# Quarters of the queries for the heads of the last two pairs: the end of a fused attention, routed feed-forward and gate kernel

## The chip, the cores and the metric

The kernel runs on one core of one Trainium2 chip. The metric is the device time of one execution in microseconds; the time before is the median of three runs.

## The reference

With x of 2048 rows (queries) and 512 columns, 32 heads of 16 values each:

```
qkv = x @ wqkv;  scores = q k^T / 4;  p = softmax(scores);  a = concat_heads(p v) @ wo
r = x @ w_r;  idx = the 2 rows of x with the largest r
y = ((silu(x[idx] @ w_gate) * (x[idx] @ w_up)) @ w_down) * sigmoid(r[idx])
b = x, with y added to the rows idx
g = sigmoid((x * gate_w).sum(-1))
out = g * a + (1 - g) * b
```

The softmax is over all 2048 keys, without a mask. The change touches the attention of the last two pairs of heads and the product with wo that follows it.

## The kernel before, in words

**Units and steps.** The heads are taken in 16 pairs. A unit is one pair and one half of the queries (1024), so there are 32 units, `u = 2 * pair + half`. A unit has 16 steps, one for each block of 128 keys: 512 steps in all. `Kx` holds the K of a pair (two buffers, by the pair's parity), `Qx` the queries of a unit (three buffers); each head has its own half of the partitions. `load_q` and `load_k` fetch them from scratch memory two units ahead (`start_step`).

**Three passes, interleaved.** For each unit the kernel first needs the largest score of each query. `m_piece` (line 546) makes one product of 128 queries by 512 keys on TensorE, 64 for a unit, and VectorE reduces them (line 560). GpSimd splits the result in a high and a low part (`pool_split`, lines 74 and 75), VectorE transposes it (line 610), and eight small transfers put it into two further rows of `Qx` (line 615), so that the scores come out with the maximum subtracted. `s_piece` (line 617) makes the scores of 128 keys by 512 queries (line 624) four times a step, and ScalarE takes their exponential (line 625). `av_mm` multiplies them by V and by a column of ones (line 633): `AV` then holds, for four blocks `ct` of (head, 512 queries), 16 rows of values and one row of sums. `av_out` copies it out at the end of a unit.

**The order** is written out by hand. While there are max products, one cycle of `ORDER` has twelve `s` (three steps), twelve `m`, three `A` (`p_v`, the value products of a step, two steps behind) and one `f`, which takes the next entry of a queue of other TensorE work (`slots`). The max products run 21 steps ahead, so they end near step 491. From step 492 on, a plain loop does four scores, one `p_v` and one entry of the queue in each step. `at_step(s, f)` hangs a function on the end of step `s`. All transfers but the indirect ones are issued by SyncE, in the order of the program.

**The output.** Heads are grouped by eight, four groups of 128 rows. For the first three, the values go to scratch, are divided by the sums and multiplied with wo in the queue (`wo_groups`). The fourth group ends with the last pair and is handled at the end. The values of pairs 12 to 14 (96 rows) go straight into `last_n`, one tile for each half of the queries. Their sums collect in `Lt`, which `l_out` inverts in eight slices on VectorE (`l_out`, line 667) and writes out; `l_last` reads them back, spread over 16 rows each, and `n_last` multiplies on GpSimd. `split_last` splits them into high and low parts (lines 524 and 525), and `wo_last` (line 534) makes one output tile of 128 queries: three matmuls (`wo_terms`, line 481) and the addition to `acc` on VectorE (`finish`, line 529). Tiles 8 to 15 do this with 96 rows, from step 497 on. For the last pair's first half (unit 30), the sums are turned and inverted by TensorE and VectorE (`l_cols` and `l_rows`, lines 684 and 693, the latter multiplied in at line 695), and its rows then join `last_n[0]`, which gives tiles 0 to 7 with all 128 rows; six of them at the ends of steps 506 to 511, two in `tail`. The last unit ends in `tail`: its sums are turned (line 721), inverted (723), spread (729, 730), turned back (733) and multiplied in (736); then eight output tiles of three matmuls each with `wz` (line 749), a copy of the last pair's rows of wo set between zeros, and for each an addition (529) and a store (532).

Of the kernel before, what the change touches and what calls it, by code (L numbers as in the profile page):

```python
# [23 lines left out]
STEPS = UNITS * KT  # L24
EL = 64


# [6 lines left out]
def gated_mix(ctx: ExitStack, tc: tile.TileContext, xT, x, wqkv, wo, w_rg, w_gate, w_up, w_down,  # L34
# [67 lines left out]
    i_scr = dram.tile([128, 1], U32, name="i_scr")  # L102
    r_scr = dram.tile([4 * 128, 128], F32, name="r_scr")


# [132 lines left out]
    def load_k(pair):  # L238

        g, r = divmod(pair * 32, 128)  # L240
        for j in range(2):
            o = (g * 128 + r + 16 * j) * S
            t = Kx[pair % 2].bitcast(F32)
            nc.sync.dma_start(t[64 * j:64 * j + 32, :], ap(qk_scr["k"], o, [[S, 16], [D * S, 2], [1, S]]).bitcast(F32))
            nc.sync.dma_start(t[64 * j + 32:64 * j + 48, :], ap(qk_scr["k"], o, [[S, 16], [1, S]]).bitcast(F32))

    def load_q(u):

        pair, half = divmod(u, 2)
        g, r = divmod(pair * 32, 128)  # L250
        n = S // 2
        for j in range(2):
            o = (g * 128 + r + 16 * j) * S + half * n
            t = Qx[u % 3].bitcast(F32)
            nc.sync.dma_start(t[64 * j:64 * j + 32, :], ap(qk_scr["q"], o, [[S, 16], [0, 2], [1, n]]).bitcast(F32))
            nc.sync.dma_start(t[64 * j + 32:64 * j + 48, :], ap(qk_scr["q"], D * S + o, [[S, 16], [1, n]]).bitcast(F32))

# [192 lines left out]
    wop = []  # L450
# [62 lines left out]

    def split_last(half, q):
        if q == 0:
            if half:
                t = ring.tile([128, 2, 1024], F32R, tag="xs", name="lahl", bufs=2)
                lastp[half] = t[:, 0], t[:, 1]
            else:
                lastp[half] = [xp.tile([128, 1024], F32R, tag=f"xl{i}", name="lahl") for i in (2, 3)]  # L520
        k = 128 if half == 0 else 96
        sl = slice(q * 512, q * 512 + 512)
        hi, lo, src = lastp[half][0][:k, sl], lastp[half][1][:k, sl], last_n[half][:k, sl]
        nc.vector.tensor_copy(hi, src)
        nc.gpsimd.tensor_sub(lo, src, hi.bitcast(F32))

# [19 lines left out]
    def m_piece(g):  # L546

        u, e = divmod(g, EL)
        t, c, j = e // 8, e // 2 % 4, e % 2
        r = g % 3  # L550
        if r == 0:
            MX[0] = mxa_tile()
        elif r == 2:
            MX[1] = mxb_tile()
        dst = MX[0][:, r] if r < 2 else MX[1]
        nc.tensor.matmul(dst, Qx[u % 3][64 * j:64 * j + 48, t * 128:t * 128 + 128],  # L556
                         Kx[(u // 2) % 2][64 * j:64 * j + 48, c * 512:c * 512 + 512], start=True, stop=True)
        if r:
            g0 = (g - 1 if r == 1 else g) % (3 * EL)
            nc.vector.tensor_reduce(Mr[:, g0:g0 + (2 if r == 1 else 1)], MX[r - 1], axis=AX.X, op=OP.max, negate=True)  # L560
# [56 lines left out]
    def s_piece(s, j, c):  # L617
        u, kt = divmod(s, KT)
        if s not in P:
            P[s] = ring.tile([128, 4, 512], F32, tag="P", name="P", bufs=3)  # L620
        k = Kx[(u // 2) % 2][64 * j:64 * j + 50, kt * 128:kt * 128 + 128]
        q = Qx[u % 3][64 * j:64 * j + 50, c * 512:c * 512 + 512]
# [4 lines left out]
    def av_mm(s):  # L627
# [3 lines left out]
        for ct in range(4):  # L631
            h = (u // 2) * 2 + ct // 2
            nc.tensor.matmul(AV[0][32 * ct:32 * ct + 32, :], V[:, kt, h * VW:h * VW + 32], P[s][:, ct, :],  # L633
                             start=kt == 0, stop=kt == KT - 1)
# [4 lines left out]
    def av_out(u):  # L639
# [24 lines left out]
    def l_out(g, i):  # L664
        n = 96 if g == 3 else 128
        sl = slice(16 * i, 16 * i + 16)
# [4 lines left out]
    def l_last(half, q):  # L671

        r = o_tile("rb", [96, 512])
        nc.sync.dma_start(r, ap(r_scr, 3 * 8 * S + half * 1024 + q * 512, [[S, 6], [0, 16], [1, 512]]))
        AV["rb", half, q] = r

    def n_last(half, q):
        a = last_n[half][:96, q * 512:q * 512 + 512]
        nc.gpsimd.tensor_mul(a, a, AV["rb", half, q])

    def l_cols(u):
        ps = mxa_tile()[:, 0, :16]
        for c in range(4):
            nc.tensor.matmul(ps[:, 4 * c:4 * c + 4], AV[u][:, c * 128:c * 128 + 128], sel_l, start=True, stop=True)
        r = ring.tile([128, 16], F32, tag="r16", name="r16", bufs=2)
        nc.vector.reciprocal(r, ps)
        AV["rx"] = o_tile("rx", [128, 16, 32])
        nc.vector.tensor_copy(AV["rx"], r[:, :, None].to_broadcast([128, 16, 32]))

    def l_rows(u):  # L690
        ps = mxa_tile()[:, 0]
        for c in range(4):
            nc.tensor.matmul(ps[:, c * 128:c * 128 + 128],
                             AV["rx"][:, 4 * c:4 * c + 4].rearrange("p a b -> p (a b)"), ident, start=True, stop=True)
        nc.vector.tensor_mul(AV[u], AV[u], ps)

    def last_rows():
        for ct in range(4):
            j, c = divmod(ct, 2)
            nc.sync.dma_start(last_n[0][96 + 16 * j:112 + 16 * j, c * 512:c * 512 + 512], AV[UNITS - 2][32 * ct:32 * ct + 16, :])  # L700

    wz = []

    def load_wz(part):
        if part == 0:
            wz.append(ring.tile([128, 2, 2, 512], F32R, tag="xs", name="wz", bufs=2))
            nc.gpsimd.memset(wz[0].bitcast(F32), 0.0)
            return
        for i in range(2):
            for ct in range(4):  # L710
                j, c = divmod(ct, 2)
                nc.sync.dma_start(wz[0][32 * ct:32 * ct + 16, i, c].bitcast(F32),
                                  wop[i][96 + 16 * j:112 + 16 * j, 3].bitcast(F32))

    def tail():
# [28 lines left out]
        for c in range(4):  # L744
            sl = slice(c * 128, c * 128 + 128)
            for k in range(2):
                ps = (st_tile, lambda: two[:, 0], st_tile, mxb_tile, st_tile, lambda: two[:, 1], st_tile, fl_tile)[2 * c + k]()
                for n, (a, b) in enumerate(((0, 0), (1, 0), (0, 1))):
                    nc.tensor.matmul(ps, hl[a][:, sl], wz[0][:, b, k, :], start=n == 0, stop=n == 2)
                finish(8 + 4 * k + c, ps)  # L750
                store(8 + 4 * k + c)

# [38 lines left out]
    def slots():  # L791
# [53 lines left out]
    at_step(400, load_wz, 0)  # L845
    at_step(404, load_wz, 1)

    def p_v(s):
# [7 lines left out]
        if u % 8 == 7 and u < 24:  # L856
            for i in range(8):
                at_step(s + 6 + i, l_out, u // 8, i)
        elif u == UNITS - 3:
            for i in range(8):  # L860
                at_step(s + 3 + i // 2, l_out, 3, i)
            for half in (1, 0):
                for q in range(2):
                    at_step(s + 10 - half, l_last, half, q)
                    at_step(s + 12 - half, n_last, half, q)
        elif u == UNITS - 2:
            at_step(s + 1, l_cols, u)
            at_step(s + 2, l_rows, u)
            at_step(s + 3, last_rows)

    def start_step(s):
        now[0] = s
        u = s // KT + 2
        if s % KT == 0 and u < UNITS:
            if u % 2 == 0 and u > 2:
                load_k(u // 2)
# [88 lines left out]
```

## Time and profile before

| | before |
|---|---|
| median of 3 runs | 1443.08 us (1442.3 to 1449.25) |
| the profiled execution | 1443.71 us, span 1441.9 us |
| TensorE busy | 1426.5 us, 99% of the span |
| VectorE busy | 1300.1 us, 90% |
| ScalarE busy | 1168.7 us, 81% |
| GpSimd busy | 302.5 us, 21% |
| mean granted TensorE clock | 0.998 |

In the profile's lines PE is TensorE, PEld its weight loads, DVE VectorE, ACT ScalarE, POOL GpSimd, and SP SyncE; a q after the name is the engine's own queue (issues and waits). A row of the timeline has its start and length in us, the engine, the line of the kernel, the operation, what is written and read, the shape and the count. In a row of groups the numbers behind the bar are the busy time in us and the mean of one in ns, then the idle time before them and what ended it. In a row of stretches the bounds and the length are followed by the busy us of PE, PEld, DVE, ACT and POOL with the count of instructions in brackets. In the chain of waits each row has a start and the share of time that the path to the end spent there.

### The profile page before, as it was taken

The numbers are of one execution on the slowest core, as the hardware profiler recorded it, in microseconds if no ns is written. First come the engines' busy times: TensorE is split into PE (matmuls) and PEld (weight loads), VectorE is DVE, ScalarE is ACT, GpSimd is POOL, SyncE is SP. The second block draws the span as 40 slices with busy tenths as digits, with TensorE's granted clock in tenths as the row PEclk, the third lists the DMA queues.
The fourth block names the chain that finished last, engine by engine and source line by source line (L and its number), as shares of the span: only waits on it lengthen the run. The fifth ranks groups of instructions, "written<-read, shape, count | busy, mean of one in ns | idle before, by whom it ended". The sixth has DMA issues, their size and how long they took to land.

```text
span 1441.9 us, 24169 instructions
## 1 busy us (share of the span) xinstructions
PE 1426.5 (99%) x9141; PEld 631.9 (44%) x9141; DVE 1300.1 (90%) x1541; ACT 1168.7 (81%) x2262; POOL 302.5 (21%) x321
## 2 busy tenths in 40 slices
PE   8999999999999999999999999999999999999998
PEld 5654444444444444444444443434444444444434
DVE  5779999999999999999999999999999999999933
ACT  4468888888888888888888888888888888888874
POOL 3652000112000001200001100033832222233220
PEclk9999999999999999999999999999999999999999
DMA  8702021212214121312222342314213121111003
GB/s 265 195 21 64 20 52 31 53 45 41 53 53 107 61 53 31 67 31 64 57 81 52 98 104 70 86 42 130 73 31 68 35 53 27 32 31 38 25 17 117
DMA packets 53475, 92.71 MB, mean 64 GB/s; under 512 B 12972, under 2 KB 24300, under 8 KB 51856
## 3 DMA queue, kind: packets, MB, share of 16 engines
q1 hardware_dynamic: 53264, 91.17, 24.4%
q8 instruction: 72, 1.18, 0.4%
q14 instruction: 43, 0.35, 0.1%
q0 software_dynamic: 96, 0.01, 0.0%
HBM read 63.64 MB, written 28.56 MB: 64 GB/s over the span
## 4 chain that ended last, share of the span: by engine, by line
PE 95%; DMA 2%; DVE 1%; SPq 1%; ACT 0%; issue 0%; POOL 0%; DVEq 0%; POOLq 0%; ACTq 0%
PE av L633 35%; PE st L624 23%; PE mxa L556 12%; PE mxb L556 10%; PE fl L150 6%; PE fl L481 4%; PE st L268 3%; DMA xs<-xT 1%; PE mxa L583 1%; DVE Mr L560 1%; DMA wvs<-wqkv 1%; PE fl L372 0%; DVE acc L529 0%; PE st L150 0%; ACT P L625 0%; SPq L615 0%
## 5 line engine op out<-in xcount | busy, mean ns | idle before, releaser
L625 ACT ACTIVATE P<-st 128x512 f32<-128x512 f32 x2028 | 1064.5, 599 | 206.9 <-PE st L624 112.9
L560 DVE TENSOR_REDUCE Mr<-mxa 128x2 f32<-128x1024 f32 x655 | 794.9, 1214 | 3.8 <-PE mxa L556 3.5
L633 PE MATMUL av<-P,V 128*32 128x512 f32 x4096 | 545.5, 605 | 0.0
L624 PE MATMUL st<-Qx,Kx 50*128 50x512 f32 x2028 | 536.2, 443 | 2.0 <-ACT P L625 2.0
L560 DVE TENSOR_REDUCE Mr<-mxb 128x1 f32<-128x512 f32 x654 | 451.9, 691 | 63.5 <-PE st L624 18.1
L624 PEld LDWEIGHTS st<-Qx,Kx 50*128 50x128 f32 x2028 | 274.6, 184 | 234.6 <-ACT P L625 215.0
L556 PE MATMUL mxb<-Kx,Qx 48*128 48x512 f32 x654 | 325.3, 497 | 0.0
L556 PE MATMUL mxa<-Kx,Qx 48*128 48x512 f32 x1310 | 296.7, 420 | 1.2 <-DVE Mr L560 1.2
L556 PEld LDWEIGHTS mxb<-Kx,Qx 48*128 48x128 f32 x654 | 119.5, 183 | 273.7 <-DVE Mr L560 254.4
L556 PEld LDWEIGHTS mxa<-Kx,Qx 48*128 48x128 f32 x1310 | 125.1, 183 | 52.2 <-DVE Mr L560 10.3
L633 PEld LDWEIGHTS av<-P,V 128*32 128x32 f32 x4096 | 80.9, 108 | 140.3 <-issue 134.7
L186 POOL TENSOR_SCALAR ev<-pe 128x512 fp32r<-128x512 f32 x24 | 35.7, 1490 | 321.3 <-ACT pe L184 321.3
L74 POOL TENSOR_SCALAR hl<-m 128x16 fp32r<-128x16 f32 x32 | 8.1, 253 | 441.1 <-DVE m L599 441.0
L448 POOL TENSOR_TENSOR acc<-acc,w 128x512 f32<-128x512 f32 x32 | 41.0, 1281 | 185.8 <-ACT w L447 171.6
L150 PE MATMUL fl<-xh,wh 128*128 128x512 f32 x96 | 42.9, 447 | 0.0
L150 PE MATMUL fl<-xh,wl 128*128 128x512 f32 x96 | 40.4, 421 | 0.0
L529 DVE SCALAR_TENSOR_TENSOR acc<-fl,gg,acc 128x512 f32<-128x512 f32 x15 | 11.3, 750 | 26.6 <-PE fl L481 26.6
L481 PE MATMUL fl<-woh,ahl 128*128 128x512 f32 x96 | 35.1, 447 | 0.0
L588 DVE TENSOR_REDUCE Mr<-mxa 128x2 f32<-128x1024 f32 x21 | 25.7, 1223 | 9.8 <-PE mxa L583 9.8
L150 PE MATMUL fl<-xl,wh 128*128 128x512 f32 x96 | 32.6, 421 | 0.0
L187 POOL TENSOR_TENSOR ev<-pe,ev 128x512 fp32r<-128x512 f32 x24 | 30.8, 1283 | 2.0
L270 ACT ACTIVATE V<-st 128x512 f32<-128x512 f32 x16 | 9.6, 598 | 25.4 <-PE st L268 25.4
(177 smaller groups left out, 781.4 us busy)
## 6 DMA issues: line engine op xcount, KB each, us to landing
Qx<-q_scr SPq DMA_DIRECT2D x62, 128.0 KB
Kx<-k_scr SPq DMA_DIRECT2D x30, 256.0 KB
k_scr<-ev SPq DMA_DIRECT2D x14, 512.0 KB
q_scr<-ev SPq DMA_DIRECT2D x14, 512.0 KB
xs<-xT SPq DMA_DIRECT2D x16, 256.0 KB
xn<-x SPq DMA_DIRECT2D x4, 1024.0 KB
Qx<-hr SPq DMA_DIRECT2D x256, 2.0 KB
acc<-x_scr SPq DMA_DIRECT2D x4, 1024.0 KB
```

Of the source, the lines that this page charges most:

```text
L150: nc.tensor.matmul(ps, a[:, i, c, :], b[nb][:, c, :], start=n == 0, stop=n == 11)
L186: nc.gpsimd.tensor_scalar(ev[:, 0], t, 1.0, None, op0=OP.mult)
L187: nc.gpsimd.tensor_sub(ev[:, 1], t, ev[:, 0].bitcast(F32))
L268: nc.tensor.matmul(ps, a[nb][:, c, sl], b[:, c, :], start=c == 0 and n == 0, stop=c == 3 and n == 2)
L448: nc.gpsimd.tensor_add(a, a, w)
L481: nc.tensor.matmul(ps, a[:, sl], b[:a.shape[0], c, :], start=first and n == 0, stop=last and n == 2)
L556: nc.tensor.matmul(dst, Qx[u % 3][64 * j:64 * j + 48, t * 128:t * 128 + 128], Kx[(u // 2) % 2][64 * j:64 * j + 48, c * 512:c * 512 + 512], ...
L560: nc.vector.tensor_reduce(Mr[:, g0:g0 + (2 if r == 1 else 1)], MX[r - 1], axis=AX.X, op=OP.max, negate=True)
L588: nc.vector.tensor_reduce(*r, axis=AX.X, op=OP.max, negate=True)
L624: nc.tensor.matmul(ps, k, q, start=True, stop=True)
L625: nc.scalar.activation(P[s][:, 2 * j + c, :], ps, AF.Exp)
L633: nc.tensor.matmul(AV[0][32 * ct:32 * ct + 32, :], V[:, kt, h * VW:h * VW + 32], P[s][:, ct, :], start=kt == 0, stop=kt == KT - 1)
```

## The change

The last four units (28 to 31; `QU = 28`) are no longer pair and half, but the four heads of pairs 14 and 15 for one quarter of the queries (512) each. A unit keeps its 64 max products, 16 steps of four scores, and value products; only which head and which queries they belong to changes. For this both pairs' K are kept: pair 14 in `Kx[0]`, pair 15 in a third tile, allocated at step 402 in a buffer that `wz` had, filled at step 406. `load_q` takes eight transfers for such a unit instead of four.

Units 28 to 30 each invert their own sums: `av_out` sends the four rows of sums into a tile of 128 x 16 and the values into rows 64 to 127 of `last_n`; `l_unit(u, 0)`, three steps later, inverts them on VectorE (one instruction of 16 columns), writes them out and reads them back spread over 64 rows; `l_unit(u, 1)`, three steps after that, multiplies them in (GpSimd; VectorE for unit 30). `split_last` then splits one quarter, all on GpSimd but for unit 30's. `l_cols`, `l_rows` and `last_rows` are gone. Pairs 12 and 13 (64 rows) take the way that 96 rows had, earlier: they end with unit 27.

In the queue, tiles 12 to 15 come first with 64 rows, then tiles 0 to 11 with all 128, in three groups of four that wait for steps 478, 494 and 505. `tail` has no tile of `last_n` left, and four output tiles with `wz` instead of eight; `wz` has half the size.

```diff
+QU = UNITS - 4
...
-            t = Kx[pair % 2].bitcast(F32)
+            t = Kx[pair % 2 if pair < PAIRS - 1 else 2].bitcast(F32)
...
+        parts = [(pair, half * S // 2, S // 2)] if u < QU else [(PAIRS - 2 + c, (u - QU) * 512, 512) for c in range(2)]
+        for i, (pair, q0, n) in enumerate(parts):
+            for j in range(2):
+                o = (pair * 32 + 16 * j) * S + q0
+                t = Qx[u % 3][:, i * n:i * n + n].bitcast(F32)
...
+    def k_of(u, c):
+        return Kx[(u // 2) % 2 if u < QU else 2 * c]
+
+    def last_k(i):
+        if i == 0:
+            Kx.append(ring.tile([128, S], F32R, tag="xs", name="Kx2", bufs=2))
+            ones(Kx[2])
+        else:
+            load_k(PAIRS - 1)
...
-    def split_last(half, q):
...
+    def split_last(quarter):
+        half, q = divmod(quarter, 2)
+        if half not in lastp:
+            t = ring.tile([128, 2, 1024], F32R, tag="xs", name="lahl", bufs=2) if half else \
+                Kx[1].rearrange("p (i n) -> p i n", i=2)
+            lastp[half] = t[:, 0], t[:, 1]
+        k = 128 if quarter < 3 else 64
         sl = slice(q * 512, q * 512 + 512)
         hi, lo, src = lastp[half][0][:k, sl], lastp[half][1][:k, sl], last_n[half][:k, sl]
-        nc.vector.tensor_copy(hi, src)
-        nc.gpsimd.tensor_sub(lo, src, hi.bitcast(F32))
+        if quarter == 2:
+            nc.vector.tensor_copy(hi, src)
+            nc.gpsimd.tensor_sub(lo, src, hi.bitcast(F32))
+        else:
+            pool_split(hi, lo, src)
...
@@ in wo_last @@
-        if half == 0:
+        if k == 128:
             store(t)
...
@@ in av_out @@
-        if pair == PAIRS - 1:
+        if u >= QU:
             AV[u] = o
+            if u == UNITS - 1:
+                return
+            Ls = AV["l", u] = ring.tile([128, 16], F32, tag="Ls", name="Ls", bufs=2)
+            for ct in range(4):
+                p = 64 * (ct % 2) + 32 * (ct // 2)
+                nc.sync.dma_start(Ls[p:p + 32, :], o[32 * ct + 16:32 * ct + 17, :])
+            half, q = divmod(u - QU, 2)
+            for ct in range(4):
+                r = 64 + 32 * (ct % 2) + 16 * (ct // 2)
+                nc.sync.dma_start(last_n[half][r:r + 16, q * 512:q * 512 + 512], o[32 * ct:32 * ct + 16, :])
             return
...
-    def l_cols(u):
...
-    def l_rows(u):
...
-    def last_rows():
...
+    def l_unit(u, i):
+        if i == 0:
+            Ls = AV.pop(("l", u))
+            nc.vector.reciprocal(Ls, Ls)
+            nc.sync.dma_start(l_scr[u - QU], Ls)
+            AV["rb", u] = o_tile("rb", [128, 512])
+            nc.sync.dma_start(AV["rb", u][64:128, :], ap(l_scr[u - QU], 0, [[512, 4], [0, 16], [1, 512]]))
+        else:
+            half, q = divmod(u - QU, 2)
+            a = last_n[half][64:128, q * 512:q * 512 + 512]
+            (nc.vector if u == UNITS - 2 else nc.gpsimd).tensor_mul(a, a, AV.pop(("rb", u))[64:128, :])
...
@@ in tail @@
-        pw = [st_tile() for _ in range(2)]
-        for t in range(2):
-            wo_terms(pw[t], lastp[0][0], lastp[0][1], 3, slice((6 + t) * 128, (7 + t) * 128), True, True)
...
-        for t in range(2):
-            finish(6 + t, pw[t])
-            store(6 + t)
-        two = mxa_tile()
-        for c in range(4):
...
+        banks = [st_tile(), mxa_tile()[:, 0], st_tile(), mxb_tile()]
+        for t in range(4):
+            for n, (a, b) in enumerate(((0, 0), (1, 0), (0, 1))):
+                nc.tensor.matmul(banks[t], hl[a][:, t * 128:t * 128 + 128], wz[0][:, b, :], start=n == 0, stop=n == 2)
+            finish(12 + t, banks[t])
+            store(12 + t)
...
@@ in slots, behind wo_groups((2,)) @@
-        yield from wait(STEPS - 15)
-        for t in range(8, 16):
-            wo_last(t, 96)
+        for t in range(12, 16):
+            wo_last(t, 64)
             yield
+        for t in range(12):
+            if t % 4 == 0:
+                yield from wait((478, 494, 505)[t // 4])
+            wo_last(t, 128)
+            yield
...
-    for q in range(2):
-        at_step(STEPS - 18 + q, split_last, 1, q)
-        at_step(STEPS - 9 + q, split_last, 0, q)
-    for t in range(6):
-        at_step(STEPS - 6 + t, wo_last, t, 128)
+    at_step(402, last_k, 0)
+    at_step(406, last_k, 1)
...
@@ in p_v, at the end of unit u @@
-        elif u == UNITS - 3:
...
-        elif u == UNITS - 2:
-            at_step(s + 1, l_cols, u)
-            at_step(s + 2, l_rows, u)
-            at_step(s + 3, last_rows)
+        elif u == QU - 1:
+            for i in range(8):
+                at_step(s + 6 + i, l_out, 3, i)
+            for i in range(4):
+                at_step(s + 16 + 2 * i, l_last, i // 2, i % 2)
+                at_step(s + 19 + 2 * i, n_last, i // 2, i % 2)
+            at_step(s + 27, split_last, 3)
+        elif QU <= u < UNITS - 1:
+            at_step(s + 3, l_unit, u, 0)
+            at_step(s + 6, l_unit, u, 1)
+            at_step(s + (13 if u == QU else 7), split_last, u - QU)
```

More of the change, by code (lines that the diff above doesn't have):

```diff
@@ L103, in gated_mix @@
     r_scr = dram.tile([4 * 128, 128], F32, name="r_scr")
+    l_scr = [dram.tile([128, 16], F32, name=f"l_scr{i}") for i in range(3)]
     W = {}
@@ L249, in load_q @@
         pair, half = divmod(u, 2)
[L250 to L256, printed above, removed]
+        parts = [(pair, half * S // 2, S // 2)] if u < QU else [(PAIRS - 2 + c, (u - QU) * 512, 512) for c in range(2)]
[3 more added lines that the diff above has]
+                t = Qx[u % 3][:, i * n:i * n + n].bitcast(F32)
+                nc.sync.dma_start(t[64 * j:64 * j + 32], ap(qk_scr["q"], o, [[S, 16], [0, 2], [1, n]]).bitcast(F32))
+                nc.sync.dma_start(t[64 * j + 32:64 * j + 48], ap(qk_scr["q"], D * S + o, [[S, 16], [1, n]]).bitcast(F32))
+    def k_of(u, c):
[6 more added lines that the diff above has]
+            load_k(PAIRS - 1)
     VP = {}
@@ L512, in gated_mix @@
     lastp = {}
-    def split_last(half, q):
[L515 to L521, printed above, removed]
+    def split_last(quarter):
[5 more added lines that the diff above has]
+        k = 128 if quarter < 3 else 64
         sl = slice(q * 512, q * 512 + 512)
         hi, lo, src = lastp[half][0][:k, sl], lastp[half][1][:k, sl], last_n[half][:k, sl]
-        nc.vector.tensor_copy(hi, src)
-        nc.gpsimd.tensor_sub(lo, src, hi.bitcast(F32))
+        if quarter == 2:
[3 more added lines that the diff above has]
+            pool_split(hi, lo, src)
     def finish(t, ps):
@@ L556, in m_piece @@
         nc.tensor.matmul(dst, Qx[u % 3][64 * j:64 * j + 48, t * 128:t * 128 + 128],
-                         Kx[(u // 2) % 2][64 * j:64 * j + 48, c * 512:c * 512 + 512], start=True, stop=True)
+                         k_of(u, t // 4)[64 * j:64 * j + 48, c * 512:c * 512 + 512], start=True, stop=True)
         if r:
@@ L631, in av_mm @@
         for ct in range(4):
-            h = (u // 2) * 2 + ct // 2
+            h = (u // 2 * 2 if u < QU else H - 4 + ct % 2 * 2) + ct // 2
             nc.tensor.matmul(AV[0][32 * ct:32 * ct + 32, :], V[:, kt, h * VW:h * VW + 32], P[s][:, ct, :],
@@ L664, in l_out @@
     def l_out(g, i):
-        n = 96 if g == 3 else 128
+        n = 64 if g == 3 else 128
         sl = slice(16 * i, 16 * i + 16)
@@ L671, in l_last @@
     def l_last(half, q):
-        r = o_tile("rb", [96, 512])
-        nc.sync.dma_start(r, ap(r_scr, 3 * 8 * S + half * 1024 + q * 512, [[S, 6], [0, 16], [1, 512]]))
+        r = o_tile("rb", [64, 512])
+        nc.sync.dma_start(r, ap(r_scr, 3 * 8 * S + half * 1024 + q * 512, [[S, 4], [0, 16], [1, 512]]))
         AV["rb", half, q] = r
     def n_last(half, q):
-        a = last_n[half][:96, q * 512:q * 512 + 512]
+        a = last_n[half][:64, q * 512:q * 512 + 512]
         nc.gpsimd.tensor_mul(a, a, AV["rb", half, q])
-    def l_cols(u):
-        ps = mxa_tile()[:, 0, :16]
-        for c in range(4):
[L684 to L688, printed above, removed]
-    def l_rows(u):
[L691 to L695, printed above, removed]
-    def last_rows():
-        for ct in range(4):
-            j, c = divmod(ct, 2)
-            nc.sync.dma_start(last_n[0][96 + 16 * j:112 + 16 * j, c * 512:c * 512 + 512], AV[UNITS - 2][32 * ct:32 * ct + 16, :])
+    def l_unit(u, i):
[9 more added lines that the diff above has]
+            (nc.vector if u == UNITS - 2 else nc.gpsimd).tensor_mul(a, a, AV.pop(("rb", u))[64:128, :])
     wz = []
@@ L705, in load_wz @@
         if part == 0:
-            wz.append(ring.tile([128, 2, 2, 512], F32R, tag="xs", name="wz", bufs=2))
+            wz.append(ring.tile([128, 2, 512], F32R, tag="w", name="wz", bufs=3))
             nc.gpsimd.memset(wz[0].bitcast(F32), 0.0)
@@ L710, in load_wz @@
             for ct in range(4):
-                j, c = divmod(ct, 2)
-                nc.sync.dma_start(wz[0][32 * ct:32 * ct + 16, i, c].bitcast(F32),
-                                  wop[i][96 + 16 * j:112 + 16 * j, 3].bitcast(F32))
+                r = 64 + 32 * (ct % 2) + 16 * (ct // 2)
+                nc.sync.dma_start(wz[0][32 * ct:32 * ct + 16, i].bitcast(F32), wop[i][r:r + 16, 3].bitcast(F32))
     def tail():
@@ L739, in tail @@
             split(hl[0][:, sl], hl[1][:, sl], o[:, sl])
-        for t in range(2):
-            finish(6 + t, pw[t])
-            store(6 + t)
-        two = mxa_tile()
[L744 to L751, printed above, removed]
+        banks = [st_tile(), mxa_tile()[:, 0], st_tile(), mxb_tile()]
[4 more added lines that the diff above has]
+            store(12 + t)
     fill, now = {}, [0]
@@ L874, in start_step @@
         if s % KT == 0 and u < UNITS:
-            if u % 2 == 0 and u > 2:
+            if u % 2 == 0 and 2 < u <= QU:
                 load_k(u // 2)
```

7 lines of the change are left out of this document (1 added, 6 removed).

## The prediction

> **What bounds the kernel now.** I read the page first, then the busy times by stretch, then the chain of waits and the timeline of the last 70 us, then SyncE's queue. The page and the stretches give the stage that the change leaves alone:
>
> ```profile
> span 1441.9 us, 24169 instructions
> L560 DVE TENSOR_REDUCE Mr<-mxa 128x2 f32<-128x1024 f32 x655 | 794.9, 1214 | 3.8 <-PE mxa L556 3.5
> L560 DVE TENSOR_REDUCE Mr<-mxb 128x1 f32<-128x512 f32 x654 | 451.9, 691 | 63.5 <-PE st L624 18.1
> ...
> 1300.00:1366.00 66.00, 66.00 (x433) 28.71 (x431) 62.91 (x79) 59.05 (x114) 20.03 (x23) 1.00 0.10 25
> ```
>
> A cycle of the written order has three steps and twelve max products; their reductions cost 4 x (1.214 + 0.691) = 7.62 us of VectorE. In the stretch before 1366 TensorE has no idle time and VectorE 5%: both are at their limit, and an operation added there costs nearly its length. The last max product runs at about 1370; what follows (steps 492 to 511, then the tail) has other limits. In the timeline each step begins with its score matmuls on line 624:
>
> ```profile
> 1372.76 0.50 PE L624 MATMUL st<-Qx,Kx 50*128 50x512 f32 x2
> ...
> 1382.88 0.73 PE L624 MATMUL st<-Qx,Kx 50*128 50x512 f32 x3
> ...
> 1396.39 0.73 PE L624 MATMUL st<-Qx,Kx 50*128 50x512 f32 x3
> ...
> 1398.94 0.73 PE L624 MATMUL st<-Qx,Kx 50*128 50x512 f32 x3
> ...
> 1406.63 0.73 PE L624 MATMUL st<-Qx,Kx 50*128 50x512 f32 x3
> ...
> 1408.29 1.00 PE L624 MATMUL st<-Qx,Kx 50*128 50x512 f32 x3
> ...
> 1411.60 0.73 PE L624 MATMUL st<-Qx,Kx 50*128 50x512 f32 x3
> ...
> 1424.41 1.92 PE L633 MATMUL av<-P,V 128*32 128x512 f32 x16
> ```
>
> Steps 492 to 496 carry no output tile: 10.12 us, 2.02 each, the pace of ScalarE's exponentials. With a tile (three matmuls on line 481) a step takes 2.56 (1396.39 to 1398.94): TensorE is the bound, and a tile costs 0.54 us. After a train of tiles one step without a tile takes 1.66 (step 505, 1406.63 to 1408.29), and the first with a tile again 3.31 (step 506, to 1411.60). The chain shows what else sits in steps 497 to 499:
>
> ```profile
> 1385.09 1.24 POOL lahl L525
> ...
> 1386.37 0.73 PE fl L481 x2
> ...
> 1389.66 0.79 PE mxa L684 x8
> ...
> 1393.00 0.89 PE mxa L693 x8
> ...
> 1396.46 0.66 PE st L624 x3
> ...
> 1397.12 0.99 PE av L633 x8
> ```
>
> The first tile of the second half waits for GpSimd's split, and unit 30's sums pass through TensorE twice, 0.79 + 0.89 us. The last two rows are the scores and the values of one step.
>
> **The last loop.** The fills are one queue, one per cycle and, from step 492, one per step. Counted in the program, the third group's pass ends in the cycle before step 489, so the waits for 478 and 494 have passed when they are reached. The order becomes tile 12 in the last cycle, 13 to 15 and 0 to 7 in steps 492 to 502, none in 503 and 504, 8 to 11 in 505 to 508, none in 509 to 511. Against before:
>
> - steps 492 to 496: 5 x 2.56 = 12.8 for 10.12, +2.7;
> - steps 497 to 504: before, 1406.63 - 1382.88 = 23.75 with eight tiles, the wait and lines 684 and 693. After, 6 x 2.56 + 1.66 + 2.02 = 19.0: -4.7;
> - steps 505 to 511, up to the last two groups of value matmuls: before 1424.41 - 1406.63 = 17.78. After, 3.31 + 3 x 2.56 + 1.66 + 2.02 + 2.02 = 16.7: -1.1.
>
> Together -3.1. Tile 12 now stands in the last cycle with maxima, but behind its last product, where the score matmuls already wait for ScalarE; the bounds are 0 and the 0.9 us of its three matmuls (0.73 for two in the chain); I take 0.2, as most of it fills that wait.
>
> **The tail.** The chain to the end:
>
> ```profile
> 1427.10 1.05 PE st L721 x8
> 1428.15 1.49 PE st L481 x6
> ...
> 1431.90 5.93 DVE acc L529 x9
> 1437.83 0.66 DVEq L961
> ```
>
> After the last reciprocals VectorE adds ten tiles at 0.66 us each, two left over and eight of the tail; this ends at 1438.49, and the span 3.4 us later. Now four are added. What they wait for, in the timeline:
>
> ```profile
> 1428.19 0.26 DVE L723 RECIPROCAL rl<-st 128x16 f32<-128x16 f32 x1 [2.92 <-PE st L721]
> ...
> 1428.53 0.42 ACT L729 ACTIVATE rxl<-rl 128x256 f32<-128x256 f32 x1 [1.49 <-DVE rl L723]
> ...
> 1429.25 0.64 PEld L733 LDWEIGHTS mxb<-cst,rxl 128*128 128x128 f32 x4
> ...
> 1431.15 0.50 PE L749 MATMUL st<-wz,onh 128*128 128x512 f32 x1 [0.62 <-ACT onh L67]
> ...
> 1431.95 0.40 PE L749 MATMUL st<-wz,onh 128*128 128x512 f32 x1
> ...
> 1432.90 0.39 PE L749 MATMUL st<-wz,onh 128*128 128x512 f32 x1
> ...
> 1433.59 0.39 PE L749 MATMUL mxb<-wz,onh 128*128 128x512 f32 x1
> ```
>
> The six matmuls on line 481 go. They cover the copies of the reciprocals, which end at 1428.95, and hold line 733's load until 1429.25: about 0.25 us is gained, not 1.49. The first tile is then complete at 1432.1 (1431.95 + 0.40 - 0.25), and TensorE gives one each 0.69 us (1432.90 to 1433.59), a little slower than VectorE adds them. The last is complete at 1434.2 and added at 1435.0: TensorE takes over as the bound and the tail loses 3.45 us rather than six adds plus the matmuls, 5.5. What follows the last add is taken as unchanged.
>
> **What is added to the stage of the maxima.** The K tile's loads and its ones are GpSimd's and SyncE's, some 20 steps before use; the splits of three quarters move to GpSimd, 30% busy there (20.03 of 66). The eight reciprocals of the sums only move earlier. Units 28 and 29 add one reciprocal each on VectorE (0.26 us, line 723). Bounds 0 and 0.5; I take 0.3, as VectorE has 5% idle.
>
> Their wait is new: VectorE takes its instructions in order, so behind it stand the reductions, and TensorE's max products behind those. The reciprocal needs four small DMAs from SyncE's queue, which now first issues eight query loads:
>
> ```profile
> L662 SPq DMA_DIRECT2D Lt<-o x120: 586/627/1171, 147.6 to 1350.7; - x120
> ...
> L660 SPq DMA_DIRECT2D an<-o x24: 517/528/563, 1140.3 to 1350.1; - x24
> ...
> 1362.74 0.33 SPq L669 DMA_DIRECT2D r_scr<-Lt  x1
> 1364.33 1.61 SPq L674 DMA_DIRECT2D rb<-r_scr  x2
> ```
>
> Counted from the start of step 464: twelve issues at 0.63 = 7.5, landing by 1.6 (1362.74 to 1364.33, a write and its landing) = 9.1. The reciprocal comes at the end of step 468, five steps of 7.62 / 3 = 12.7. Cover 3.6 us; for unit 29 it is larger. Cost 0.
>
> **The chain of unit 30.** Quarter 2 (tiles 8 to 11) hangs on it. More rows that it needs:
>
> ```profile
> 1378.10 1.60 SPq L674 DMA_DIRECT2D rb<-r_scr  x2
> ...
> 1393.93 0.69 DVE L695 TENSOR_TENSOR o<-o,mxa 128x512 f32<-128x512 f32 x1
> ...
> 1404.85 0.42 DVE L524 CAST lahl<-an 128x512 fp32r<-128x512 f32 x1
> ```
> ```profile
> 1378.92 4.81 DMA rb<-r_scr
> ```
>
> From the start of step 497 the copy of its sums ends at 2.5 (0.66 scores, 1.0 values, 0.69). The reciprocal stands behind tile 5's add at the end of step 500, 11.1, then 0.26 and 1.6 to write it out: 13.0. The read back of 64 rows is bounded by nothing and by the pair of 96-row reads, 5.6 us (1378.10 to 1383.73); a single smaller one I put, as an estimate, at two thirds, 3.7. Multiply 0.69, cast 0.42, GpSimd 1.24: 19.1. Tile 8 needs it at 6 x 2.56 + 3.68 + 1.66 = 20.7. Slack 1.6: cost 0, at most 0.3 with the whole 5.6, and 1 us for each us beyond.
>
> **The clock in the tail.** The six matmuls also kept TensorE at work. Three equal stretches near the start:
>
> ```profile
> 22.85:26.26 3.41, 1.82 (x9) 1.00 (x7) 2.74 (x4) 3.04 (x6) 1.27 (x1) 1.00 0.84 212
> ...
> 29.67:33.08 3.41, 1.43 (x7) 0.57 (x5) 2.78 (x4) 1.16 (x2) 0.00 (x0) 1.00 0.78 198
> 33.08:36.50 3.42, 3.42 (x9) 2.58 (x9) 2.57 (x4) 0.00 (x0) 0.00 (x0) 0.50 0.87 215
> ```
>
> The last three columns are the granted clock and the transfers. With 1.82 us of TensorE's work in 3.41 the clock stayed; after 1.43 it was halved for the next stretch, which held 9 matmuls. In the new tail the last value matmul ends at 1426.33 (1424.41 + 1.92), the first tile begins at 1430.9 (1431.15 - 0.25), and between lie only line 721 (1.05 us) and line 733 (about 1, an estimate from the 0.64 of its first four loads). A stretch of 3.41 us there has between 1 and 2 us of work, on both sides of those rows. If the clock halves, nine of the twelve last matmuls take 3.41 us instead of 2.07 (0.23 each, a third of 0.69): +1.3. Where the boundaries of the stretches fall the trace can't tell, so I take 0 and keep 1.3 for the range. [...]
>
> **The sum.** -3.1 + 0.2 - 3.45 + 0.3 = -6.05 us, taken as -6.1. The profiled execution took 1443.71 us (span 1441.9), 0.6 above the median of 1443.08; from the median this gives 1437.0. A change of 0.5%, about what a measurement of this kernel can tell from none, is 7.2 us.
>
> **Rivals.** *The clock halves in the tail*: 1437.0 + 1.3 = 1438.3. For it the 1.43 us row; against it that the stretches must fall just so. *Unit 30's chain is late*, TensorE waits before tile 8 as it did at 1386.37: a read and write slower by 2 to 5 us gives 0.4 to 3.4 us, about 1439. For it the 4.81 us in the chain, against it that only one read is under way. *The end is cheaper*: with four stores instead of ten in the last stretch, the 3.4 us after the last add may shrink by the 0.66 of one store's turn, and the 0.5 added to VectorE and the last cycle may hide wholly: 1437.0 - 1.2 = 1435.8, just over 0.5%. *VectorE waits for the sums of units 28 and 29*: if SyncE's queue, which stands still for each write that must land before its read, brings them later than the cover, each us stops the maxima. It is slower than before when the two together are 6.05 us past their covers, and by over 0.5% from 13.3 us on, 1450.3; at 8 us in all it gives 1445. Against it: the sums are first of their unit in the queue. *That it does not do what it says*, tiles 0 to 3 coming in steps 478 on, cannot be: the fill queue is in the third group's pass then.
>
> **How the numbers follow.** Forecast 0.48 (own range 1435.5 to 1438.5), clock 0.15, late chain 0.12, cheaper end 0.14, VectorE's wait 0.11. The range keeps all but the last and reaches a little past the late chain and the cheaper end: 1434.0 to 1442.0. Faster by over 0.5%: the cheaper end and a quarter of the forecast, which its spread puts beyond 1435.9, 0.26. Slower by over 0.5%: of VectorE's wait the part past 13.3 us, 0.08, since a queue that lags once lags for both units. Same: the rest, 0.66.
>
> **What would show it.** In the changed profile: steps 492 to 502 at 2.56 us, no idle time before tile 13 or 8; two tile-less steps 503 and 504; four adds at about 0.69 at the end, each waiting for TensorE; no idle time of VectorE before the new reciprocals; the granted clock 1.00 until the last tile. It is wrong if the cycles before step 489 take longer than 7.7 us, or if TensorE waits at step 505.

## The result, and the profile after

The changed kernel takes 1437.49 us (median of 8 executions, 1436.71 to 1438.9), the one before 1443.65 on the same chip: ratio 0.995, 95% interval 0.9937 to 0.9964. The forecast was 1437.0, with a change of less than 0.5% as the likeliest case; the interval reaches to both sides of 0.5%. The profiled execution took 1437.04 us, with a span of 1435.2. Behind the number two terms were off in opposite directions, and the traces show both.

First the landmarks: ScalarE's copies of the finished units 27, 28, 29 and 31, in the timeline of before and then of the changed kernel.

```profile
1263.75 0.60 ACT L646 ACTIVATE o<-av 128x512 f32<-128x512 f32 x1 [0.16 <-PE av L633]
...
1305.12 0.60 ACT L646 ACTIVATE o<-av 128x512 f32<-128x512 f32 x1
...
1345.70 0.60 ACT L646 ACTIVATE o<-av 128x512 f32<-128x512 f32 x1
...
1426.45 0.60 ACT L646 ACTIVATE o<-av 128x512 f32<-128x512 f32 x1 [2.00 <-issue]
```
```profile
1262.58 0.60 ACT L663 ACTIVATE o<-av 128x512 f32<-128x512 f32 x1
...
1304.04 0.60 ACT L663 ACTIVATE o<-av 128x512 f32<-128x512 f32 x1
...
1344.66 0.60 ACT L663 ACTIVATE o<-av 128x512 f32<-128x512 f32 x1
...
1421.50 0.60 ACT L663 ACTIVATE o<-av 128x512 f32<-128x512 f32 x1 [1.21 <-PE av L650]
```

The changed kernel is 1.17 us ahead at unit 27, where the two programs hardly differ yet. This is not the change: the copy of the first unit already comes 1.52 us earlier (at 145.14, before 146.66), and in the traces of this study it lies anywhere between 144.8 and 147.0 us, whichever kernel it is. From there on (step 492 begins at 1372.76 before, at 1371.40 after; the last value matmuls end at 1426.33 and 1421.43):

| stretch | before | changed | difference | forecast |
|---|---|---|---|---|
| unit 27's copy to unit 29's | 81.95 | 82.08 | +0.13 | +0.3 |
| unit 29's copy to step 492 | 27.06 | 26.74 | -0.32 | +0.2 |
| step 492 to the last value matmul | 53.57 | 50.03 | -3.54 | -3.1 |
| last value matmul to the end of the span | 15.57 | 13.77 | -1.80 | -3.45 |

**The last loop** gained more than forecast. TensorE's timeline of the changed kernel (line 495 is the output tile, 641 the scores, 650 the values):

```profile
1371.40 0.73 PE L641 MATMUL st<-Qx,Kx 50*128 50x512 f32 x3
...
1372.06 1.07 PE L650 MATMUL av<-P,V 128*32 128x512 f32 x8
1373.06 0.50 PE L495 MATMUL fl<-woh,lahl 64*128 64x512 f32 x1
1373.07 0.49 PE L641 MATMUL st<-Qx,Kx 50*128 50x512 f32 x1
...
1374.48 1.07 PE L650 MATMUL av<-P,V 128*32 128x512 f32 x8
...
1376.84 1.07 PE L650 MATMUL av<-P,V 128*32 128x512 f32 x8
...
1379.19 1.07 PE L650 MATMUL av<-P,V 128*32 128x512 f32 x8
...
1381.75 1.07 PE L650 MATMUL av<-P,V 128*32 128x512 f32 x8
```

The steps with the 64-row tiles (13 to 15) take 2.42, 2.36 and 2.35 us from value product to value product; with tile 0 (128 rows) it is the 2.56 of the forecast. The rows at 1373.06 and 1373.07 suggest why: a 64-row matmul of the tile and a score matmul (50 rows, in the other half of the rows) start within 0.01 us of each other. The run with 128 rows, below, tests it.

**The tail** gained half of what was forecast. The 3.41 us stretches of TensorE's clock there (after the sum and the busy time of PE, PEld, DVE, ACT and POOL come the granted clock, the DMA share and GB/s), and then TensorE's timeline:

```profile
1416.91:1420.32 3.41, 3.41 (x28) 1.00 (x21) 0.00 (x0) 3.33 (x7) 0.00 (x0) 1.00 0.02 5
1420.32:1423.74 3.42, 2.17 (x20) 1.15 (x15) 0.41 (x2) 0.74 (x2) 0.00 (x0) 1.00 0.00 0
1423.74:1427.15 3.41, 2.86 (x10) 2.23 (x10) 1.39 (x5) 1.10 (x3) 0.00 (x0) 0.50 0.00 0
1427.15:1430.56 3.41, 3.41 (x9) 2.68 (x9) 1.86 (x3) 0.00 (x0) 0.00 (x0) 0.50 0.20 76
```
```profile
1418.65 2.78 PE L650 MATMUL av<-P,V 128*32 128x512 f32 x24
1422.15 1.05 PE L739 MATMUL st<-cst,o 128*128 128x4 f32 x8 [0.72 <-ACT o L663]
1424.06 1.22 PE L748 MATMUL mxb<-cst,rxl 128*128 128x128 f32 x4 [0.86 <-ACT rxl L744]
...
1428.00 0.63 PE L758 MATMUL mxa<-wz,onh 128*128 128x512 f32 x1
1428.43 0.63 PE L758 MATMUL mxa<-wz,onl 128*128 128x512 f32 x1
...
1430.56 0.40 PE L758 MATMUL mxb<-wz,onh 128*128 128x512 f32 x1
1430.81 0.39 PE L758 MATMUL mxb<-wz,onl 128*128 128x512 f32 x1
```

The granted clock is halved 2.3 us after the last value matmul, for two stretches: the matmuls on line 758 come 0.43 us apart and go back to 0.23 only at 1430.6. It is the rival to which the prediction gave 0.15. The stretch ahead of the drop had TensorE at work for 2.17 us: 1.11 us of value products and the 1.05 of line 739, whose matmuls have 4 columns each.

### The profile page after: what moved, and what is told of

Its sections match the earlier page's. It is cut to its first block, busy times and chain, and to the rows that moved or that the text cites. A ratio compares the mean times of both kernels' runs of the same rounds, so it can differ in the third digit from the quotient of the medians.

```text
span 1435.2 us, 24154 instructions
## 1 busy us (share of the span) xinstructions
PE 1423.6 (99%) x9113; PEld 630.2 (44%) x9113; DVE 1295.4 (90%) x1535; ACT 1169.7 (82%) x2262; POOL 312.0 (22%) x328
## 4 chain that ended last, share of the span: by engine, by line
PE 96%; DMA 2%; DVE 1%; ACT 0%; SPq 0%; issue 0%; ACTq 0%; DVEq 0%
PE av L650 35%; PE st L641 23%; PE mxa L573 12%; PE mxb L573 10%; PE fl L153 6%; PE fl L495 4%; PE st L282 3%; DMA xs<-xT 1%; PE mxa L600 1%; DMA wvs<-wqkv 1%; PE fl L386 0%; PE st L153 0%; DVE Mr L577 0%; DMA k_scr<-Qx 0%; ACT P L642 0%; PE fl L424 0%
## 5 line engine op out<-in xcount | busy, mean ns | idle before, releaser
L282 PE MATMUL st<-Kx,xh 128*128 128x512 f32 x64 | 28.1, 440 | 0.0
```

The costliest lines, as they stand in the source:

```text
L282: nc.tensor.matmul(ps, a[nb][:, c, sl], b[:, c, :], start=c == 0 and n == 0, stop=c == 3 and n == 2)
```

## The experiments

Each is the changed kernel, or the one before, with a small edit. The spare matmuls of the first two go to a bank of PSUM (where the matmuls write) that nobody reads; the second `keep` stands between line 739 and the reciprocal.

### Cover for the clock

```diff
 def tail():
+    cover = fl_tile()
+    def keep(n):
+        for _ in range(n):
+            nc.tensor.matmul(cover, lastp[0][0][:, :128], wop[0][:, 3, :], start=True, stop=True)
+    keep(3)
     ...
+    keep(3)
     nc.vector.reciprocal(r, ps)
```

> The changed kernel with six matmuls of 512 columns added in the tail, three ahead of the last sums' turn and three behind it, into a PSUM bank that nobody reads. Theory A (the clock): the changed kernel's tail runs at half clock from about 2.3 us after its last value matmul, so its tiles come 1.28 us apart; with the cover the granted clock stays 1.00, the tiles come 0.69 apart, and the kernel is 1.2 to 1.7 us faster than the changed one, ratio to before about 0.994 to 0.995. Rival B (the tail's pace has another reason, for instance the weights' rows or the banks): the pace stays at 1.28 and the time is the same or up to 0.5 us longer. Rival C (the cover delays the sums' turn): the clock stays, but the turn begins up to 0.7 us later, and the gain is under 1 us.

Measured: 1435.58 us (1434.15 to 1436.18), ratio 0.9931 (0.9914 to 0.9948). The clock stays in the tail, and the tiles come 0.69 us apart. The stretches of this run:

```profile
1420.24:1423.65 3.41, 3.35 (x23) 2.04 (x16) 0.55 (x2) 1.01 (x2) 0.00 (x0) 1.00 0.00 0
1423.65:1427.06 3.41, 2.78 (x15) 2.09 (x16) 2.12 (x5) 0.75 (x2) 0.00 (x0) 1.00 0.00 0
```

Theory A holds for the clock, and rival C falls: line 739's counterpart starts 0.75 us after the last value matmul, as without the cover. How much time the cover is worth is another matter, below, where the changed kernel runs on the same chip.

### Busy time or columns

The same with eleven matmuls of 4 columns instead of six of 512:

```diff
-            nc.tensor.matmul(cover, lastp[0][0][:, :128], wop[0][:, 3, :], start=True, stop=True)
+            nc.tensor.matmul(cover[:, :4], lastp[0][0][:, :128], wop[0][:, 3, :4], start=True, stop=True)
-    keep(3)
+    keep(5)
     ...
-    keep(3)
+    keep(6)
```

> The changed kernel with eleven matmuls of 4 columns in the tail (five ahead of the last sums' turn, six behind it) where the run with the cover had six of 512 columns. In the rows they take about the same busy time as the cover, but hardly any columns pass. Theory A1 (the clock is granted by what streams through TensorE, not by the busy time of the rows): the clock still halves in the tail, the tiles come 1.28 us apart in part, and the time is that of the changed kernel, up to 0.3 us longer. Rival A2 (busy time counts): the clock stays 1.00 in the tail and the time is that of the run with the cover, 1.2 to 1.9 us below the changed kernel.

Measured: 1438.18 us (1435.96 to 1439.83), ratio 0.995 (0.9935 to 0.9965): the changed kernel's time.

```profile
1422.30:1425.71 3.41, 3.23 (x28) 2.27 (x19) 0.55 (x2) 0.98 (x2) 0.00 (x0) 1.00 0.00 0
1425.71:1429.13 3.42, 3.11 (x10) 2.48 (x11) 1.50 (x4) 0.86 (x3) 0.00 (x0) 0.50 0.00 0
1429.13:1432.54 3.41, 3.41 (x9) 2.63 (x9) 1.62 (x4) 0.00 (x0) 0.00 (x0) 0.50 0.20 77
```

TensorE's rows are busy for 3.23 of 3.41 us, 0.86 of it the last value products and the rest in matmuls of 4 columns, and the clock is halved all the same. Busy time is not what keeps it (A2 falls); six matmuls of 512 columns in the same two places did.

### The same gap in the kernel before

```diff
-        pw = [st_tile() for _ in range(2)]
-        for t in range(2):
-            wo_terms(pw[t], lastp[0][0], lastp[0][1], 3, slice((6 + t) * 128, (7 + t) * 128), True, True)
...
-            finish(6 + t, pw[t])
```

> The kernel before, with the two left-over tiles' six matmuls and two additions in the tail left out (tiles 6 and 7 miss the last group's term). Theory A: without them the tail's clock falls as in the changed kernel; about nine of the 24 last matmuls run at half pace, which costs 1.5 to 2 us and takes back what the two additions (1.33 us) and the earlier turn (0.25) give: 0 to -0.3 us against before, granted clock 0.50 in part of the tail. Rival B (the six matmuls have nothing to do with the clock): the clock stays and the kernel is 1.3 to 1.6 us faster.

Measured: 1445.15 us (10 executions), ratio 1.0003 (0.999 to 1.0017): work of 1.6 us taken out, and no gain. The interval runs from 1.4 us faster to 2.5 slower, so it is the trace that tells the theories apart:

```profile
1426.47:1429.88 3.41, 1.80 (x15) 1.36 (x12) 0.55 (x2) 1.01 (x2) 0.00 (x0) 1.00 0.61 231
1429.88:1433.29 3.41, 3.20 (x11) 2.36 (x11) 1.60 (x4) 0.83 (x2) 0.00 (x0) 0.50 0.00 0
```

The clock is halved, as theory A said; with the two tiles it stayed at 1.00 up to the last matmul in the trace of the kernel before. So the two leftover tiles also served as cover, and removing them, as the change does, opens the gap.

### The changed kernel and the cover on one chip

> The changed kernel itself again, on the same chip as the two that follow, as their base. About 1437.5 us, ratio to before 0.995; the granted clock at half for one or two stretches of the tail, and the last tiles 1.28 us apart there.

> The changed kernel with the six cover matmuls of 512 columns, again. Theory A: the clock stays in the tail, 1.4 to 2.0 us below the changed kernel of this call, ratio to before about 0.993. Rival (the first difference came from the executions' own starts, which differ by up to 2 us): within 0.5 us of the changed kernel.

Measured on this other chip: the changed kernel 1434.78 us (five executions), ratio 0.9945 (0.9932 to 0.9959); with the cover 1434.73, ratio 0.9942 (0.9928 to 0.9955). No difference: theory A's number is missed, and so is the halved clock expected of the changed kernel. The rival's number came (within 0.5 us), but its reason, the starts, does not explain the first difference: the first unit's copy came at 145.14 us in the first trace of the changed kernel and at 145.21 in the one with the cover, while their tails, from the last value matmul on, took 13.77 and 11.52 us. The trace of the changed kernel here says more:

```profile
1419.45:1422.86 3.41, 2.44 (x24) 1.18 (x16) 0.21 (x1) 0.84 (x2) 0.00 (x0) 1.00 0.00 0
1422.86:1426.27 3.41, 2.17 (x11) 1.64 (x12) 1.90 (x6) 1.16 (x3) 0.00 (x0) 1.00 0.00 0
1426.27:1429.69 3.42, 2.28 (x10) 1.50 (x8) 2.84 (x4) 0.00 (x0) 0.00 (x0) 1.00 0.45 170
```
```profile
1418.05 2.78 PE L650 MATMUL av<-P,V 128*32 128x512 f32 x24
...
1428.15 0.40 PE L758 MATMUL mxb<-wz,onh 128*128 128x512 f32 x1
```

The boundaries of the stretches fall 2.03 and 5.45 us after the last value matmul (1420.83), and the gap is shared out between two stretches; in the first trace one fell at 2.31, and the stretch ahead of it ended with little. From 1420.83 to the end of this span (1432.4) it is 11.57 us: 2.2 less than the 13.77 with the clock halved, and 4.0 less than before. The second of these stretches has the same 2.17 us of busy rows as the one that lost the clock in the first trace, but 1.16 us of it are line 748's matmuls of 128 columns and 1.01 line 758's of 512.

Three edits further down leave the tail as it is, and each of their traces has one stretch at half clock. In the one with the early reciprocals the boundary falls 2.96 us after the last value matmul, about as in the first run with the cover (2.81):

```profile
1423.89:1427.30 3.41, 1.77 (x18) 1.23 (x11) 0.55 (x2) 1.01 (x2) 0.00 (x0) 1.00 0.00 0
1427.30:1430.71 3.41, 3.18 (x11) 2.42 (x11) 1.60 (x4) 0.83 (x2) 0.00 (x0) 0.50 0.00 0
```

With the wide tiles the stretch ahead of the drop had 1.84 us of busy rows, and with unit 30 late 1.93. From the last value matmul to the end of the span these three take 12.47, 12.40 and 13.04 us: 0.8 to 1.5 us more than with the clock kept.

Of the 13 executions of the changed kernel, the eight with a mean granted clock of 0.996 took 1436.65 to 1438.9 us, the four with 0.998 or more on this chip 1434.2 to 1435.2; one, on the first chip, had 0.998 and 1437.14. The eleven with the cover took 1433.97 to 1436.18. The mean is only a sign, as it also counts halved stretches near the start: the trace with the cover here has 0.997 and none in the tail. So the cover keeps the clock in both of its traces, and it gains nothing where the boundaries fall well. Why they fell well in about four of five executions here and in at most one of eight there is open.

### One reciprocal instead of the turn

```diff
-        for c in range(4):
-            nc.tensor.matmul(ps[:, 4 * c:4 * c + 4], o[:, c * 128:c * 128 + 128], sel_l, start=True, stop=True)
...
+        for t in range(2):
+            nc.tensor.matmul(pr[t], selb.rearrange("p a b -> p (a b)"), o[:, 256 * t:256 * t + 256], start=True, stop=True)
...
+            nc.vector.reciprocal(rc[:, sl], pr[t])
+            nc.vector.tensor_mul(o[:, sl], o[:, sl], rc[:, sl])
```

> As the run with the cover, and the last unit's sums are spread over the 32 rows of their block by one matmul with a constant 0/1 matrix (two halves of 256 columns, the matrix made by ScalarE at step 405), then inverted on VectorE over 256 columns and multiplied in; the turn, the small reciprocal, its two copies and the turn back are gone. In the run with the cover the stretch from the copied sums to the first multiplied half was 3.2 us (1421.51 to 1424.72). Theory: two matmuls of about 0.45, a reciprocal of 256 columns at about 0.42 (the pace of VectorE's other operations on 256 columns) and a product of 0.42, the second half behind it: 1.5 to 2.2 us in all, 0.8 to 1.4 us faster than the run with the cover. Rival (the reciprocal takes several times as long for an element as a product): no gain, or slower by up to 1 us.

Measured: 1438.97 us (1437.3 to 1439.23), ratio 0.9968 (0.9955 to 0.998): 4.2 us slower than the run with the cover. It has six cover matmuls too. VectorE's timeline:

```profile
1424.11 1.76 DVE L752 RECIPROCAL rc<-mxb 128x256 f32<-128x256 f32 x1 [8.42 <-PE mxb L747]
1425.97 0.42 DVE L753 TENSOR_TENSOR o<-o,rc 128x256 f32<-128x256 f32 x1
```

The rival is right about the reciprocal, though the loss is larger than its 1 us: 1.76 us for 256 columns, against 0.26 for 16, is about 6 ns a column, four times a product's. TensorE then waits longer, and the clock was halved here too, later in the tail. From the last value matmul to the end it takes 14.39 us, against 11.55 in the trace with the cover on the same chip; how the 2.8 us are shared between reciprocal and clock is not shown.

### 64 rows or 128

```diff
+        if quarter == 3:
+            for x in lastp[1]:
+                nc.gpsimd.memset(x[64:128, 512:1024].bitcast(F32), 0.0)
...
-            wo_last(t, 64)
+            wo_last(t, 128)
```

> The changed kernel with tiles 12 to 15 made with all 128 rows, the upper 64 set to zero by GpSimd. In the changed kernel, steps 492 to 494 took 2.36 to 2.41 us where 2.56 were forecast. Theory: a matmul on 64 rows runs beside the score matmuls of the other half of the rows; with 128 rows the steps go back to 2.56, and the last cycle gets longer by up to 0.5 us: 0.5 to 1.1 us slower than the changed kernel. Rival (the steps are shorter because ScalarE has work in store, or because the 64-row load is shorter): the steps stay at 2.4, no change.

Measured: 1438.3 us (1436.92 to 1439.18), ratio 0.9954 (0.9937 to 0.9972).

```profile
1372.82 1.07 PE L653 MATMUL av<-P,V 128*32 128x512 f32 x8
...
1375.37 1.07 PE L653 MATMUL av<-P,V 128*32 128x512 f32 x8
...
1377.94 1.07 PE L653 MATMUL av<-P,V 128*32 128x512 f32 x8
...
1380.49 1.06 PE L653 MATMUL av<-P,V 128*32 128x512 f32 x8
```

The three steps take 2.55, 2.57 and 2.55 again. Step 492 to the last value matmul takes 50.69 us (50.03 with 64 rows): the theory holds. That the load of 64 rows is shorter is no rival: line 495's loads take 0.18 to 0.19 us with either shape in the changed kernel's trace. The stretch from unit 29's copy to step 492 stays at 26.78, so tile 12 in the last cycle is hidden with either shape.

### The wait for the sums

```diff
-            at_step(s + 3, l_unit, u, 0)
+            at_step(s + (1 if u < UNITS - 2 else 3), l_unit, u, 0)
```

> The changed kernel with the reciprocals of units 28 and 29 two steps earlier, one step after the copy of the sums instead of three. Theory (VectorE stands in order behind the wait, and each us of it stops the maxima): the sums land about 2.8 us after the reciprocal of unit 28 could start and about 1.8 us after that of unit 29; VectorE shows these waits in front of the reciprocals, and the kernel is 3 to 4.6 us slower than the changed one. Rival (VectorE's slack and the two banks take the wait up): under 1 us. In both, the three steps of the change hide the wait wholly, and no reading of the transfers is late.

Measured: 1440.18 us (1438.4 to 1442.84), ratio 0.9969 (0.9956 to 0.9983).

```profile
1308.49 0.25 DVE L712 RECIPROCAL Ls<-Ls 128x16 f32<-128x16 f32 x1 [1.39 <-DMA Ls<-o]
...
1350.56 0.25 DVE L712 RECIPROCAL Ls<-Ls 128x16 f32<-128x16 f32 x1 [1.45 <-DMA Ls<-o]
```

The waits are 1.39 and 1.45 us (2.8 and 1.8 were expected), and unit 28's copy to unit 31's takes 120.42 instead of 117.46 us: +2.96 for 2.84 of waiting. So each us does stop the maxima, just under the low end of the theory, and the rival is refuted. The three steps of the change cover it: its trace has no such wait.

### Unit 30's chain one step later

```diff
-            at_step(s + 3, l_unit, u, 0)
+            at_step(s + (3 if u < UNITS - 2 else 4), l_unit, u, 0)
```

> The changed kernel with unit 30's reciprocal one step later (four steps after the copy of the sums instead of three); the product, the split and the tiles stay where they are. In the changed kernel GpSimd's split for tile 8 ended 0.9 us before the second matmul of tile 8 needed it. Theory (the chain has about 0.9 us to spare, and each us beyond is a wait of TensorE in step 505): the reciprocal comes 2.56 us later, TensorE waits 1.5 to 1.9 us for tile 8, and the kernel is 1.2 to 1.9 us slower than the changed one. Rival (the read back overlaps less when later, or the stores ahead of it in SyncE's queue add to it): 3 us or more. Rival (the reciprocal isn't what ends last in the chain): under 0.5 us.

Measured: 1438.57 us (1437.35 to 1439.52), ratio 0.9957 (0.9942 to 0.9971).

```profile
1406.48 0.50 PE L495 MATMUL fl<-woh,lahl 128*128 128x512 f32 x1
1407.83 0.50 PE L495 MATMUL fl<-woh,lahl 128*128 128x512 f32 x1 [0.84 <-POOL lahl L540]
```

TensorE waits for GpSimd's split inside tile 8; unit 29's copy to unit 31's takes 78.13 us instead of 76.84, +1.3, at the low end of the theory. The reciprocal comes 2.54 us later, counted from unit 29's copy, but the product behind it only 2.14. The changed kernel does not wait there.

### The sums that passed through TensorE

```diff
-            at_step(s + 1, l_cols, u)
-            at_step(s + 2, l_rows, u)
```

> The kernel before without lines 684 and 693 and what hangs on them: unit 30's sums are not turned, inverted or multiplied in (its rows join the last group undivided). Theory (TensorE bounds these steps, so its 0.79 + 0.89 us are the cost): 1.6 to 1.8 us faster than before. Rival (the steps are held by ScalarE as well): under 0.8 us.

Measured: 1442.57 us (10 executions), before 1444.15, ratio 0.9991 (0.9979 to 1.0002). In the trace unit 29's copy to unit 31's takes 78.69 us instead of 80.75: 2.06 less, where the rows of lines 684 and 693 add up to 1.68. So the theory holds in the trace, a little above its size; the medians differ by 1.6 us, but their interval still includes no change.

## Why the prediction was right, point by point

- *The last loop* (-3.1, measured -3.54). The order of the tiles, the 2.56 us of a step with a tile and the cost of lines 684 and 693 were as worked out. So was the sum of the two empty steps and the one behind them, though not its parts: the second empty step took 2.41 us instead of 2.02, the first one with a tile 2.85 instead of 3.31. The term that was mis-sized is tiles 13 to 15: taken at the price of 96 and 128 rows, they cost about 0.2 us less each. With 128 rows the loop is 50.69, -2.9.
- *Tile 12 and the reciprocals of the sums* (+0.2 and +0.3, measured -0.32 and +0.13). Tile 12 is hidden. The eight reciprocals "only move earlier": they now lie ahead of unit 29's copy instead of behind it, so the two rows share a shift, and their sum, -0.2 against +0.5, is the fair comparison.
- *The tail* (-3.45, measured -1.80). With the clock kept it is -4.0: TensorE takes over from VectorE at 0.69 us a tile as said, and from the last add (1429.34) to the end of the span (1432.4) it is 3.1 us instead of 3.4, half of the 0.66 us that the rival of the cheaper end gave for it.
- *The clock* is the step that failed, in its chance and its price. The prediction took the busy time of the rows for what holds the clock, drew the line between 1.43 and 1.82 us, and put the term at 0; but 2.17 us were not enough in the first trace, 1.84 not in that of the wide tiles, and the 3.23 of the run with 4 columns neither. Line 721's 1.05 us (line 739 now) counted for much less than that time, as the run with 4 columns shows. The price was 2.2 us in the first trace, not 1.3, because a second stretch followed at half clock, and the turn back on line 748 was slowed too; with one stretch it was 0.8 to 1.5, so 1.3 was a fair middle. On the first chip it happened in seven or eight of eight executions, by their mean clock. The Trainium skill (TensorE: Matmul & The Clock Gate, Part 1) ties the drop to an idle window of about 3.4 us; in this tail the longest gap ahead of the drop is 0.7 us, so as a gap of that length it does not fit the measurement.
- *The sum.* The tail lost 1.65 us against the forecast; the loop, the last cycle and the reciprocals gave 1.1 back. By the terms the traces gain 5.53 us against the 6.05 of the sum; the medians differ by 6.16, and a difference of 0.6 us is within what the starts of the executions vary. That 1437.49 lies 0.5 us from 1437.0 is partly luck: with the clock kept in most executions, on the other chip, the same kernel is at 1434.8, a ratio of 0.9945, beyond the 0.5%, though its interval (0.9932 to 0.9959) reaches back over it.
- *VectorE's wait and unit 30's chain* did not happen; the two delays by design show that both were priced rightly (about 1 us for each us of wait) and that the covers are real. Unit 30's is thinner than the 1.6 us of the forecast: the product came 2.14 us later for a loss of 1.3, which leaves 0.8 to 0.9.

## What to carry to other kernels

Work that is taken out of a stretch where TensorE mostly waits can be what holds its clock: price the matmuls behind the gap at both paces, and where the gap is as short as here (some 4 us), try filling it with wide matmuls that nobody reads. The busy time of the rows does not tell whether the clock stays: here matmuls of 4 columns did not hold it, and matmuls of 512 in their place did. Take several executions, as the outcome depends on where the stretches fall. A reciprocal or a product placed on an engine that works in order needs its transfer landed, and here a step number was a sound way to buy that cover.

## What the runs showed of the hardware that was not expected

- Matmuls on 64 rows run beside matmuls on the other half of the rows: three tiles cost about 0.2 us less each, and the gain vanishes when zeros fill the upper rows (2.55 to 2.57 us a step instead of 2.35 to 2.42).
- The granted clock is decided in stretches of 3.41 us. One with 3.23 us of busy rows, 2.4 of them in 4-column matmuls, was followed by half clock; one with 1.82 us of 512-column matmuls was not. What exactly counts is open: 1.43 us of 512-column matmuls did not hold it near the start of the kernel before, while 1.39 us of value products together with 1.05 us of 4-column matmuls did (1419.45 to 1422.86 in the trace of the other chip).
- VectorE's reciprocal takes 1.76 us for 256 columns from PSUM, a product 0.42.
